# Batch 0's set-up in two halves of the heads, gathers issued earlier, and batch 0's squares and output product moved to the next phase, in a fused attention and snake-activation kernel

## The chip, the cores and the metric

The kernel runs on one core of a Trainium2 chip. The metric is the device time of one execution in microseconds (us). Before the change three runs gave 392.09, 391.79 and 391.86 us, a median of 391.86.

Five engines work side by side, each through its own instructions in order, and wait for each other by semaphores: TensorE (PE in the profile; its weight loads are PEld), VectorE (DVE), ScalarE (ACT), GpSimd (POOL) and SyncE (SP). POOL and SP also issue the transfers (DMAs): POOL those that cast float32 to bfloat16 on the way or that gather rows by an index, SP the others. PE writes its results to PSUM (eight banks of 2 KB on each of 128 partitions); ACT and DVE read them there.

## The reference

```python
# q, k, v: (8 batches, 8 heads, 576 positions, 64); global_idx: 8 sorted positions
scores = scale * np.matmul(q, k.transpose(0, 1, 3, 2))
mask = np.abs(pos[:, None] - pos[None, :]) <= 32          # window
mask = mask | is_global[:, None] | is_global[None, :]     # 8 global positions see and are seen by all
scores = np.where(mask, scores, -1000000000.0)
attn = exp(scores - max); attn = attn / (sum + 1e-09)
x = (attn @ v), heads side by side                        # (4608, 512)
h = x @ w_in                                              # (512, 2048)
s = np.sin(alpha * h)
g = h + s * s / (alpha + 1e-09)
out = g @ w_out                                           # (2048, 512), float32
```

## The kernel before

Everything runs in an order written out by hand; no scheduler moves an instruction. The work goes batch by batch: attention of batch b (`attention`), then the first product with its activation (`gemm1`), and the second product (`gemm2`) spread in single matmuls over the phases behind it, by `fill(n)`: n matmuls of the oldest waiting `gemm2` are put on PE at the place of the call. `phase_a(b+1, b)` is attention of batch b+1 beside the second product of batch b.

*Attention.* 576 positions are 12 tiles of 48. `KX` holds, for each pair of heads and each tile, a 128x128 stationary matrix: the first head's keys in rows and columns 0 to 63, the second's in 64 to 127, zeros elsewhere, and in each half 48 own keys and the 8 global ones. `QX` holds the queries in segments of 52 (4 global, 48 own), with padding; `VX` the values like the keys. All three exist twice, for even and odd batches, and the zeros are written once. For each pair of heads and each group of four tiles `scores` makes four matmuls into a PSUM tile of two (`ring`), ACT takes the exponential (L732) and DVE multiplies by `MASK` (L735). `products` (L766) makes the numerators (with `VX`, into zn) and the denominators (with the blocks of ones `OB`, into zd); `inverse` takes a logarithm L (L792) and an exponential R (L795) on ACT; `sums` reduces the parts of the global queries; `normalise` writes xT (L798). The products of pair hp-1 stand between the scores of pair hp.

*gemm1.* 16 groups nt of 128 columns: eight matmuls (L942), the sine on ACT (L976), its square on ACT or DVE (L981, L983), and H on DVE (L987). The PSUM tiles zn, zr and zd take turns. In batches 0 and 1, groups 10 to 13 also place the next batch's keys and queries (`place`, eight pairs of DVE copies, L348 and L355).

*Set-up of batch 0.* POOL loads k and q of batch 0 as 96 rows (8 heads x 12) of 48x64 values each, with a cast (L443). PE turns them 48 times (L583) into six PSUM tiles of one bank; each tile's copies into `KX` and `QX` (`place_part`, L599 and L604) belong to one engine, ACT or DVE in turn. The rows at the global positions come by three gathers on POOL (L520), with row numbers that DVE computes (`grow`). The mask is made on 64 partitions from small index tiles of POOL, and copied to the other 64 (L570). DVE clears KX[0], ACT QX[0], POOL VX[0] in two halves between the V loads (L525).

*Loads.* On POOL, in this order: V of batch 0, pairs 0 and 1; w_in, row blocks 0 and 1; V, pairs 2 and 3; w_in, blocks 2 and 3; the cast of batch 1's k and q into DRAM (`cast_qk`), which SP later loads turned (`turn_qk`, L338). In batch 0's attention, after pair 0 (`beside(0)`): POOL clears VX[1]; `gather_v` puts eight loads on SP (global rows of V of all batches) and their cast on POOL (L676); `gather_kq` puts eight gathers on POOL (L663), global rows of k and q of all batches; DVE clears KX[1] and QX[1] after pairs 1 and 2 (L1067). `turn_kq` turns the gathered rows on PE ahead of group 9 of batch 0's gemm1 (L684). At group 10 POOL waits (`seen`) for the turned q of batch 1, then loads V of batch 1 with the placing of its globals (L364, L369) behind pair 0, and w_out between pairs 1 and 2. POOL's loads use eight semaphores in turn, so that each waits for the one eight before it.

*Squares.* For a check of the sine's range the kernel sums the squares of x (`square_x`, L873 to L878) and of w_in (`square_w`, L847, L849), on DVE beside the attention of the following batch.

Of the kernel before, what the change touches and what calls it, by code (L numbers as in the profile page):

```python
# [10 lines left out]
ALU = mybir.AluOpType  # L11
# [5 lines left out]
P = 128  # L17
# [230 lines left out]
def kernel(  # L248
# [166 lines left out]
    nat = {w: H2[0:KW, 2 + 3 * w : 5 + 3 * w, :].rearrange("p n c -> p (n c)")[:, 0 : KT * D] for w in (0, 1)}  # L415
    gkq = [H2[:, 14, w * 256 : (w + 1) * 256].rearrange("p (n t d) -> p n t d", n=2, t=2) for w in (0, 1)]
    gv = H2[0 : NG * B, 15, 0 : 2 * H * D].bitcast(DT.float32).rearrange("p (h d) -> p h d", d=D)

    setup = tc.alloc_tile_pool(name="setup", bufs=1)

    g64 = setup.tile([NG * B, 1], DT.int64, name="g64")
    gidx8 = setup.tile([D, NG], DT.int64, name="gidx8")
    gp64 = setup.tile([D, 1], DT.int64, name="gp64")
    for t in (gidx8, gp64):
# [5 lines left out]
    nc.sync.dma_start(out=gp64[KT : KT + NG], in_=global_idx[:, None])  # L430
    nc.sync.dma_start(
        out=gidx8[KT : KT + NG],
        in_=bass.AP(tensor=global_idx.tensor, offset=global_idx.offset, ap=[[0, NG], [1, NG]]),
    )
    nc.sync.dma_start(out=girow[:], in_=global_idx[None, :])
    with nc.allow_non_contiguous_dma("2048 elements once"):
        nc.sync.dma_start(out=alphaT[:], in_=moe_alpha.rearrange("(t p) -> p t", p=P))

    prow = setup.tile([P, 1], DT.int32, name="prow")
    nc.gpsimd.iota(prow[:], pattern=[[0, 1]], base=0, channel_multiplier=1)  # L440
    make_identity(nc, identb[:])
    for w, src in ((1, k), (0, q)):
        nc.gpsimd.dma_start(out=nat[w], in_=src[0].rearrange("h (i r) d -> (h i) (r d)", r=KT))  # L443
    kpos = setup.tile([D, 1], DT.float32, name="kpos")
    odd = setup.tile([D, 1], DT.float32, name="odd")
    nc.gpsimd.memset(odd[:], float(KT - 1))

    nc.gpsimd.iota(kpos[:], pattern=[[0, 1]], base=0, channel_multiplier=2,
                   allow_small_or_imprecise_dtypes=True)
    nc.gpsimd.affine_select(  # L450
        out=odd[:], in_=odd[:], compare_op=ALU.is_ge, fill=0.0, base=-(KT // 2),
        channel_multiplier=1, pattern=[[0, 1]],
    )

    nc.gpsimd.affine_select(
        out=odd[:], in_=odd[:], compare_op=ALU.is_ge, fill=-4096.0, base=KT - 1,
        channel_multiplier=-1, pattern=[[0, 1]],
    )
    nc.gpsimd.tensor_tensor(out=kpos[:], in0=kpos[:], in1=odd[:], op=ALU.subtract)
    qrel = setup.tile([D, 2, 2, WCOL // 2], DT.float32, name="qrel")  # L460
    for par, left in ((0, PAD), (1, 40)):
        nc.gpsimd.iota(qrel[:, par, :, 0:left], pattern=[[1, 2], [2, left]], base=-WIN,
                       channel_multiplier=0, allow_small_or_imprecise_dtypes=True)
        nc.gpsimd.iota(qrel[:, par, :, left:60], pattern=[[1, 2], [2, 60 - left]],
                       base=2 * left - 40, channel_multiplier=0, allow_small_or_imprecise_dtypes=True)
    qpos = setup.tile([D, NT12, 2, 24], DT.float32, name="qpos")
    nc.gpsimd.iota(qpos[:], pattern=[[KT, NT12], [1, 2], [2, 24]], base=0, channel_multiplier=0,
                   allow_small_or_imprecise_dtypes=True)


    later = setup.tile([D, NG], DT.float32, name="later")
    nc.gpsimd.memset(later[:], 0.0)
    nc.gpsimd.affine_select(
        out=later[:], in_=later[:], compare_op=ALU.is_gt, fill=1.0,
        base=-KT, channel_multiplier=1, pattern=[[-1, NG]],
    )
    isg = setup.tile([D, 1], DT.float32, name="isg")
    nc.gpsimd.memset(isg[:], 1.0)
    for base, sgn in ((-KT, 1), (KT + NG - 1, -1)):
        nc.gpsimd.affine_select(  # L480
            out=isg[:], in_=isg[:], compare_op=ALU.is_ge, fill=0.0, base=base,
            channel_multiplier=sgn, pattern=[[0, 1]],
        )
    gi32 = girow[:].bitcast(DT.int32)
    greg = [nc.sync.value_load(gi32[0:1, 2 * j : 2 * j + 1], min_val=0, max_val=S - 1) for j in range(NG)]

    nc.scalar.preload_act_table_set("natural_log_exp_and_others")
    nc.scalar.activation(
        out=QX[0][:].rearrange("p h y c -> p (h y c)"),
        in_=identb[:, 0:1].to_broadcast([P, NHP * 2 * QROW]), func=AF.Copy, scale=0.0,  # L490
    )
    nc.vector.memset(KX[0][:], 0.0)
    rowi = setup.tile([P, 2], DT.int32, name="rowi")
    rowf = setup.tile([P, 4], DT.float32, name="rowf")
    nc.vector.tensor_scalar(out=rowi[:, 0:1], in0=prow[:], scalar1=B - 1, scalar2=None, op0=ALU.bitwise_and)
    nc.vector.tensor_scalar(
        out=rowi[:, 1:2], in0=prow[:], scalar1=NG * B, scalar2=None, op0=ALU.bitwise_and
    )
    nc.vector.tensor_copy(out=rowf[:, 0:2], in_=rowi[:])
    for m in range(2):  # L500
        nc.vector.tensor_copy(
            out=rowf[m * NG * B : (m + 1) * NG * B, 2:3], in_=g64[:].bitcast(DT.int32)[:, 0:1]
        )

    nc.vector.scalar_tensor_tensor(
        out=rowf[:, 3:4], in0=rowf[:, 0:1], scalar=float(S), in1=rowf[:, 2:3], op0=ALU.mult, op1=ALU.add
    )
    nc.vector.tensor_copy(out=grow[:], in_=rowf[0 : NG * B, 3:4])
    nc.vector.memset(ones[:], 1.0)
# [3 lines left out]
    nc.vector.memset(OB[D:P, D:P], 1.0)  # L513


# [19 lines left out]
    nc.scalar.activation(out=qrel[:], in_=qrel[:], func=AF.Square, bias=kpos[:, 0:1], scale=-1.0)  # L535
    band = setup.tile([D, 2, 2, WCOL // 2], DT.bfloat16, name="band")
# [3 lines left out]
    nc.vector.memset(band[0:KT, 0, :, PAD : PAD + 4], 1.0)  # L540
    nc.vector.memset(band[0:KT, 1, :, 40:44], 1.0)
    M2 = MASK[:].rearrange("p (t e) c -> p t e c", e=2)
    nc.vector.tensor_copy(
        out=M2[0:D], in_=band[:].rearrange("p e x c -> p e (x c)")[:, None].to_broadcast([D, 6, 2, WCOL])
    )

    gpf = setup.tile([D, 1], DT.float32, name="gpf")
    nc.vector.tensor_copy(out=gpf[:], in_=gp64[:].bitcast(DT.int32)[:, 0:1])
    nc.scalar.activation(out=qpos[:], in_=qpos[:], func=AF.Square, bias=gpf[:, 0:1], scale=-1.0)
    gf = setup.tile([D, NG], DT.float32, name="gf")  # L550
    nc.vector.tensor_copy(out=gf[:], in_=gidx8[:].bitcast(DT.int32)[:, 0::2])
    first = setup.tile([D, NG], DT.float32, name="first")
    nc.vector.tensor_scalar(
        out=first[:], in0=gf[:], scalar1=gpf[:, 0:1], scalar2=None, op0=ALU.not_equal
    )

    nc.vector.tensor_tensor(out=first[:], in0=first[:], in1=later[:], op=ALU.max)
    fone = setup.tile([D, 1], DT.float32, name="fone")
    nc.vector.tensor_reduce(out=fone[:], in_=first[:], axis=AX.X, op=ALU.min)
    nc.vector.tensor_tensor(out=fone[:], in0=fone[:], in1=isg[:], op=ALU.mult)  # L560
    far = setup.tile([D, NT12, 2, 24], DT.bfloat16, name="far")
# [5 lines left out]
    for e, c0 in ((0, 20), (1, 16)):  # L567
        own = M2[0:D, :, e].rearrange("p t (x c) -> p t x c", x=2)[:, :, :, c0 : c0 + 24]
# [5 lines left out]
    turnp = tc.alloc_tile_pool(name="turnp", bufs=1, space=PSUM)  # L574
    small = tc.alloc_tile_pool(name="small", bufs=1, space=PSUM)
    part, pg = {}, {}
    NA = NH // 3
    for w, name in ((1, "k"), (0, "q")):
        for n in range(3):
            part[w, n] = turnp.tile([P, NA, P], DT.bfloat16, name=f"t{name}{n}")  # L580
            for a in range(NA):
                r = (n * NA + a) * P
                nc.tensor.transpose(  # L583
                    out=part[w, n][:, a, 0:KW], in_=nat[w][:, r : r + P], identity=identb[0:KW, 0:KW]
                )
        pg[w] = small.tile([D, NG * B], DT.bfloat16, name="pg" + name)
        nc.tensor.transpose(
            out=pg[w][:], in_=g0[name][:], identity=identb[0 : NG * B, 0 : NG * B]
        )
    act, dve = nc.scalar.copy, nc.vector.tensor_copy  # L590

    def place_part(w, n, copy):
        for t in range(2):
            rows = slice(t * D, (t + 1) * D)
            for y in range(2):
                src = part[w, n][y * D : (y + 1) * D, :, 0:KW]
                if w == 1:
                    c = t * D + y * NH + n * NA
                    copy(  # L599
                        out=KX[0][rows, :, :, c : c + NA],  # L600
# [99 lines left out]
    def attention(b, beside):  # L700
# [105 lines left out]
        for hp in range(NHP):  # L806
# [4 lines left out]
            if hp:  # L811
                products(hp - 1, (0, 1))
# [340 lines left out]
```

## Time and profile before

| what | value |
|---|---|
| median of three runs | 391.86 us |
| the profiled execution | 392.27 us |
| its span, first to last instruction | 390.5 us |
| PE busy | 340.1 us (87%) |
| DVE busy | 294.6 us (75%) |
| ACT busy | 285.6 us (73%) |
| POOL busy | 137.9 us (35%) |
| mean granted clock of PE | 0.972 |
| batch 0: first scores / first sine | 18.2 / 38.8 us |
| batch 1: first scores / first gemm1 matmul | 63.3 / 85.1 us |
| batch 2: first scores | 108.5 us |

The page cuts the span into 40 slices of 9.76 us; a digit is the busy share of a slice in tenths. A row of the timeline gives start, duration, engine, line, operation, output and inputs, shape, and count; in brackets stands how long the engine was idle ahead of it and what ended that. A row of the windows gives the stretch, its length, PE's busy time (and instructions), the clock that PE was granted as a share of full speed, the DMA engines' share and GB/s. Busy time includes overlapping parts of merged rows, so of matmuls that follow each other the distance between starts tells more than the duration of one.

### The profile page before, as it was taken

The page shows a single profiled execution, that of the slowest core. Times are in us where ns is not written, and L with a number is a line of the kernel's source. Part 1 is how long each engine was busy: PE and PEld are TensorE (multiplying, and loading weights), DVE is VectorE, ACT ScalarE, POOL GpSimd, SP SyncE. Part 2 cuts the span into 40 slices and gives each one's busy share as a digit, 9 for nine tenths or more (in the row PEclk, how much of TensorE's full clock was granted, in tenths as well). Part 3 has the DMA queues.
Part 4 walks back from the last instruction along what each step waited for, and adds up shares of the span by engine and source line. Part 5 has one row for each costly group of instructions (what it writes and reads, how often), then busy time and mean ns, then how long its engine had stood idle before and what let it go on. Part 6 is the DMA issues. An engine that isn't in the chain of part 4 may idle for free. (4 is left out here: it accounts for less than half of the span.)

```text
span 390.5 us, 8393 instructions
## 1 busy us (share of the span) xinstructions
PE 340.1 (87%) x3060; PEld 234.1 (60%) x3107; DVE 294.6 (75%) x599; ACT 285.6 (73%) x552; POOL 137.9 (35%) x219
## 2 busy tenths in 40 slices
PE   2378775999798899999999999999999999899892
PEld 1377543566555576666666666667676766676341
DVE  7967769577969978888888887888788876689400
ACT  6767858668977578778888888788888888675110
POOL 7963795646746600571047203750000000000001
PEclk9985989999999899999999999999999999999997
DMA  7799969999999957488646983644411001101221
GB/s 121 43 163 219 144 47 179 156 150 190 158 140 107 185 108 148 72 77 156 123 71 68 162 127 65 61 56 90 89 44 39 2 27 56 29 2 31 59 75 48
DMA packets 104011, 37.94 MB, mean 97 GB/s; under 512 B 96122, under 2 KB 98170, under 8 KB 103514
## 3 DMA queue, kind: packets, MB, share of 16 engines
q0 software_dynamic: 56224, 18.70, 42.9%
q1 hardware_dynamic: 47738, 18.63, 24.7%
q8 instruction: 26, 0.43, 0.5%
q14 instruction: 23, 0.19, 0.2%
HBM read 37.15 MB, written 17.83 MB: 141 GB/s over the span
## 5 line engine op out<-in xcount | busy, mean ns | idle before, releaser
L1000 PE MATMUL zo<-w_out,H 128*128 128x512 bf16 x529 | 142.3, 379 | 2.7 <-DMA w_out<-in_moe_w_out_dram 0.7
L942 PEld LDWEIGHTS <-w_in 128*128 128x128 bf16 x1024 | 100.5, 99 | 49.7 <-issue 18.5
L386 POOL DMA_DIRECT2D VX<-in_v_dram x128 | 83.5, 664 | 109.3 <-PE zd L766 82.6
L732 ACT ACTIVATE E<-ring 128x480 bf16<-128x480 f32 x96 | 54.3, 568 | 33.7 <-PE ring L724 33.1
L1000 PEld LDWEIGHTS <-H 128*128 128x128 bf16 x576 | 51.8, 97 | 39.2 <-issue 0.8
L942 PE MATMUL zn<-xT,w_in 128*128 128x288 bf16 x384 | 59.2, 292 | 4.8 <-DVE H L987 4.0
L735 DVE TENSOR_TENSOR E<-E,MASK 128x480 bf16<-128x480 bf16 x96 | 36.2, 409 | 19.3 <-ACT E L732 18.1
L942 PE MATMUL zr<-xT,w_in 128*128 128x288 bf16 x320 | 48.9, 289 | 2.0 <-DVE H L987 1.2
L976 ACT ACTIVATE sb<-zn,alphaT 128x576 bf16<-128x576 f32 (+1 forms) x48 | 35.6, 741 | 19.5 <-PE zn L942 15.5
L987 DVE SCALAR_TENSOR_TENSOR H<-s,recipT,zn 128x576 bf16<-128x576 bf16 x48 | 39.1, 814 | 13.3 <-ACT s L981 9.7
L942 PE MATMUL zd<-xT,w_in 128*128 128x288 bf16 x320 | 46.6, 285 | 2.4 <-DVE H L987 2.4
L1028 POOL DMA_INDIRECT out_dram<-osb,grow x1 | 1.0, 1002 | 125.8 <-SPq L1121 125.8
L724 PE MATMUL ring<-QX,KX 128*128 128x120 bf16 x384 | 37.3, 223 | 8.1 <-DVE QX L604 4.5
L981 ACT ACTIVATE s<-sb 128x576 bf16<-128x576 bf16 (+1 forms) x62 | 42.7, 689 | 2.0
L724 PEld LDWEIGHTS <-KX 128*128 128x128 bf16 x384 | 28.2, 101 | 22.5 <-issue 11.2
L987 DVE SCALAR_TENSOR_TENSOR H<-s,recipT,zd 128x576 bf16<-128x576 bf16 x40 | 32.5, 814 | 7.0 <-ACT s L981 5.3
L766 PEld LDWEIGHTS <-VX 128*128 128x128 bf16 x448 | 28.0, 102 | 15.4 <-issue 10.0
L987 DVE SCALAR_TENSOR_TENSOR H<-s,recipT,zr 128x576 bf16<-128x576 bf16 x40 | 32.5, 813 | 4.7 <-ACT s L981 2.4
L983 DVE TENSOR_TENSOR s<-sb 128x576 bf16<-128x576 bf16 (+1 forms) x66 | 30.7, 465 | 6.3 <-ACT sb L976 6.0
L1006 ACT COPY osb<-zo 128x512 f32<-128x512 f32 x36 | 20.8, 578 | 19.9 <-PE zo L1000 19.9
L976 ACT ACTIVATE sb<-zd,alphaT 128x576 bf16<-128x576 f32 (+1 forms) x40 | 29.7, 742 | 7.5 <-PE zd L942 5.1
L766 PE MATMUL zn<-E,VX 128*128 128x120 bf16 (+2 forms) x336 | 28.2, 213 | 6.7 <-DVE xT L798 6.7
(158 smaller groups left out, 449.7 us busy)
## 6 DMA issues: line engine op xcount, KB each, us to landing
VX<-in_v_dram POOLq DMA_DIRECT2D x128, 36.0 KB, 3.3
kd<-in_k_dram POOLq DMA_DIRECT2D x7, 576.0 KB, 9.5
qd<-in_q_dram POOLq DMA_DIRECT2D x7, 576.0 KB, 10.5
w_in<-in_moe_w_in_dram POOLq DMA_DIRECT2D x4, 512.0 KB, 7.4
w_out<-in_moe_w_out_dram POOLq DMA_DIRECT2D x4, 512.0 KB, 9.2
out_dram<-osb SPq DMA_DIRECT2D x8, 256.0 KB
out_dram<-osb SPq DMA_DIRECT2D x8, 224.0 KB
out_dram<-osb SPq DMA_DIRECT2D x8, 192.0 KB
```

The source lines that it names most:

```text
L386: nc.gpsimd.dma_start(out=VX[b % 2][r : r + 24, hp, :, t * D : t * D + D], in_=v[b, 2 * hp + t].rearrange("(i a y) d -> y a i d", a=24, y= ...
L724: nc.tensor.matmul(out=ps[:, e * WCOL : (e + 1) * WCOL], lhsT=kx[:, hp, i, :], rhs=qx[:, hp, :, s0 : s0 + 60], start=True, stop=True, skip ...
L732: nc.scalar.activation(out=Eg, in_=ps[:, 0 : 4 * WCOL], func=AF.Exp, scale=scale, accum_out=EA[:, n : n + 1])
L735: nc.vector.tensor_tensor(out=Eg, in0=Eg, in1=MASK[:, 4 * g : 4 * g + 4, :].rearrange("p i c -> p (i c)"), op=ALU.mult,)
L766: nc.tensor.matmul(out=out_t[:, half, :, a - half * CUT : z - half * CUT], lhsT=OB[:] if key else VXb[:, hp, i, :], rhs=E[:, i, :, a - s0 ...
L942: nc.tensor.matmul(out=h[:, e, 0:HALF], lhsT=lhsT, rhs=xT[:, c, e, :], start=(c == 0), stop=(c == CT - 1), skip_group_check=True,)
L976: nc.scalar.activation(out=sb[:, :, 0:W], in_=h[:, :, 0:W], func=AF.Sin, scale=alphaT[:, nt : nt + 1])
L981: nc.scalar.activation(out=s2[:, :, 0:W], in_=sb[:, :, 0:W], func=AF.Square)
L983: nc.vector.tensor_tensor(out=s2[:, :, 0:W], in0=sb[:, :, 0:W], in1=sb[:, :, 0:W], op=ALU.mult)
L987: nc.vector.scalar_tensor_tensor(out=dst.rearrange("p (e c) -> p e c", e=2), in0=s2[:, :, lo:hi], scalar=recipT[:, nt : nt + 1], in1=h[:, ...
L1000: nc.tensor.matmul(out=ops[:], lhsT=H2[:, nt, blk * P : (blk + 1) * P], rhs=w_out[:, nt, :], start=(nt == 0), stop=(nt == NT - 1),)
L1006: nc.scalar.copy(out=osb[:], in_=ops[:])
```

## The change

Set-up: k and q of batch 0 are loaded and turned in halves of four heads (partitions 0 to 47 and 64 to 111), issued first on POOL. Each half fills 24 columns of 128 rows in two banks (zn, zd, zn again, zo). The first half is placed at once, t = 0 by ACT and t = 1 by DVE; the second by `second_half`, after pair 0's scores, three quarters by ACT. The mask is made on 128 partitions, and its index columns on DVE. VX[0] is cleared by ACT, KX[0] by DVE in halves; alpha comes as 16 rows and is turned on PE. Ten matmuls of ones are put ahead of the first transposes.

Loads: the gathers of batch 0 stand right behind the index tiles; w_in comes in four blocks of 512 columns; the cast of batch 1 stands between the second and third. After pair 0 POOL clears QX[1], and `gather_kq` stands ahead of the cast of the values and of the clearing of VX[1]; DVE clears KX[1] in four pieces. `seen` reads the turned k, and V of pairs 1 and 2 of batch 1 goes ahead of w_out.

Attention: in batch 0 the denominators of a pair stand ahead of scores(hp, 2) and the numerators behind it. A matmul of ones follows each group of scores of pairs 1 to 3 of batch 0 and 0 to 2 of batch 1. In batch 1 `fill` puts its matmuls (64 in all) behind pair 3 and into gemm1, and the squares of batch 0's x and of two row blocks of w_in go to groups 3, 4, 6 and 8 of batch 1's gemm1.

```diff
-    def load_w_in(cs):
-        for c in cs:
-            nc.gpsimd.dma_start(out=w_in[:, c, :], in_=moe_w_in[c * P : (c + 1) * P, :])
+    def load_w_in(gs):
+        for g in gs:
+            cols = slice(g * DFF // 4, (g + 1) * DFF // 4)
+            nc.gpsimd.dma_start(
+                out=w_in[:, :, cols], in_=moe_w_in[:, cols].rearrange("(c p) n -> p c n", p=P)
+            )
...
+    for half in range(2):
+        for w, src in ((1, k), (0, q)):
+            nc.gpsimd.dma_start(
+                out=nat[w][D * half : D * half + HK],
+                in_=src[0, HH * half : HH * half + HH].rearrange("h (i r) d -> (h i) (r d)", r=KT),
+            )
...
-    for w, src in ((1, k), (0, q)):
-        nc.gpsimd.dma_start(out=nat[w], in_=src[0].rearrange("h (i r) d -> (h i) (r d)", r=KT))
...
+    clear(QX[0][:].rearrange("p h y c -> p (h y c)").bitcast(DT.float32))
...
+    clear(vflat[:, 0:half])
...
+    def warm(z, n):
+        for _ in range(n):
+            nc.tensor.matmul(
+                out=z[:], lhsT=ones[:], rhs=ones[:][:, None, :].to_broadcast([P, 4, P]),
+                start=True, stop=True, skip_group_check=True,
+            )
+    warm(zo[0], 10)
...
-    for hps in ((0, 1), (2, 3)):
-        nc.gpsimd.memset(VX[0][:, hps[0] : hps[1] + 1].bitcast(DT.int32), 0)
-        if hps[0] == 0:
-            load_v(0, hps)
-    load_w_in((0, 1))
-    load_v(0, (2, 3))
-    load_w_in((2, 3))
-    cast_qk(1)
+    nc.scalar.activation(out=qrel[:], in_=qrel[:], func=AF.Square, bias=kpos[:, 0:1], scale=-1.0)
+    clear(vflat[:, half : 2 * half])
+    load_v(0, (0,))
+    load_w_in((0,))
+    load_v(0, (1, 2))
+    load_w_in((1,))
+    load_v(0, (3,))
+    cast_qk(1)
+    load_w_in((2, 3))
     load_vg(0)
...
+    def turn_part(w, half, z):
+        part[w, half] = z[:].bitcast(DT.bfloat16)[:, :, 0 : NH // 2 * HK].rearrange("p n (a c) -> p n a c", c=HK)
+        rows = slice(D * half, D * half + HK)
+        for a in range(NH):
+            nc.tensor.transpose(
+                out=part[w, half][:, a // 12, a % 12], in_=nat[w][rows, a * P : (a + 1) * P],
+                identity=identb[rows, rows],
+            )
...
+    turn_part(1, 0, zn)
+    for y in range(2):
+        place_part(1, 0, 0, y, act)
+        place_part(1, 0, 1, y, dve)
+    turn_part(0, 0, zd)
+    gpf = setup.tile([P, 1], DT.float32, name="gpf")
...
     nc.scalar.activation(out=qpos[:], in_=qpos[:], func=AF.Square, bias=gpf[:, 0:1], scale=-1.0)
+    for y in range(2):
+        place_part(0, 0, 0, y, act)
+        place_part(0, 0, 1, y, dve)
...
+    turn_part(1, 1, zn)
...
+    turn_part(0, 1, zo2)
+    for t, copy in ((0, act), (1, dve)):
+        place_global_keys(t, copy)
+        place_global_queries(t, copy)
+    nc.vector.tensor_copy(out=alphaT[:], in_=both[:, 0:NT])
...
-    nc.vector.tensor_copy(out=MASK[D:P], in_=MASK[0:D])
...
+    def second_half():
+        for w in (1, 0):
+            for t, y, copy in ((0, 0, act), (0, 1, act), (1, 0, act), (1, 1, dve)):
+                place_part(w, 1, t, y, copy)
...
+        def idle(hp):
+            if (b == 0 and hp) or (b == 1 and hp < 3):
+                warm(zo[0], 1)
...
                 scores(hp, g)
                 fill(per_scores[hp][g])
-            if hp:
+                idle(hp)
+            if b == 0 and hp:
+                products(hp - 1, range(3), (1,))
+            elif hp:
                 products(hp - 1, (0, 1))
             scores(hp, 2)
+            idle(hp)
+            if b == 0 and hp:
+                products(hp - 1, range(3), (0,))
+            elif hp:
+                products(hp - 1, (2,))
             if hp:
-                products(hp - 1, (2,))
                 inverse(hp - 1)
...
+            if b == 1 and nt in (3, 4):
+                square_x(0, nt - 3)
+            if b == 1 and nt in (6, 8):
+                square_w(nt // 2 - 3)
             if b == 0 and nt == 10:
-                nc.gpsimd.tensor_copy(out=seen[:], in_=turned[1][0][0:1, 0:1])
+                nc.gpsimd.tensor_copy(out=seen[:], in_=turned[1][1][0:1, 0:1])
                 load_v(1, (0,))
                 place_globals(1)
-                load_v(1, (1,))
+                load_v(1, (1, 2))
                 load_w_out()
-                load_v(1, (2, 3))
+                load_v(1, (3,))
...
-            fill(PER_GROUP[nt])
+            fill((GROUP_LATE if b == 1 else PER_GROUP)[nt])
...
-    LATE = ((0, 0, 0), (2, 6, 4), (6, 6, 6), (6, 6, 8))
+    LATE = ((0, 0, 0), (0, 0, 0), (0, 0, 0), (4, 4, 6))
     MIDST = 4
     PER_GROUP = (0, 0, 5) + 11 * (1,) + (0, 0)
+    GROUP_LATE = (0, 0, 4) + 10 * (3,) + (4, 4, 4)
...
                 if at == 0:
-                    nc.gpsimd.memset(VX[1][:].bitcast(DT.int32), 0)
+                    second_half()
+                    nc.gpsimd.memset(QX[1][:].bitcast(DT.int32), 0)
                     gather_v()
                     gather_kq()
+                    cast_globals_v()
+                    nc.gpsimd.memset(VX[1][:].bitcast(DT.int32), 0)
                     turn_qk(1)
-                if 1 <= at < 3:
-                    nc.vector.memset((KX, QX)[at - 1][1][:], 0.0)
+                if at >= 0 and at < NHP:
+                    nc.vector.memset(KX[1][:, at], 0.0)
                 return
...
-            if 0 <= at < 2:
+            if 0 <= at < 2 and b_moe:
                 square_x(b_moe, at)
...
-            if b_moe < 2 and at in (2, 3):
-                square_w(2 * b_moe + at - 2)
+            if b_moe == 1 and at in (2, 3):
+                square_w(at)
```

More of the change, by code (lines that the diff above doesn't have):

```diff
@@ L450 @@
[L450 to L482, printed above, removed]
+    nc.sync.dma_start(out=girow[:], in_=global_idx[None, :])
+    arow = setup.tile([NT, P], DT.float32, name="arow")
+    for t in (0, D):
+        nc.sync.dma_start(out=gp64[t + KT : t + KT + NG], in_=global_idx[:, None])
+        nc.sync.dma_start(
+            out=gidx8[t + KT : t + KT + NG],
+            in_=bass.AP(tensor=global_idx.tensor, offset=global_idx.offset, ap=[[0, NG], [1, NG]]),
@@ L545 @@
     )
-    gpf = setup.tile([D, 1], DT.float32, name="gpf")
+    small = tc.alloc_tile_pool(name="small", bufs=1, space=PSUM)
+    both = small.tile([P, 512], DT.float32, name="pg")
+    act, dve = nc.scalar.copy, nc.vector.tensor_copy
+    part = {}
+    def turn_part(w, half, z):
[5 more added lines that the diff above has]
+                identity=identb[rows, rows],
+            )
@@ L577 @@
[L577 to L588, printed above, removed]
-        )
@@ L689, in turn_kq @@
             )
-    banks = mctx.enter_context(tc.tile_pool(name="banks", bufs=1, space=PSUM))
-    zn, zd = [banks.tile([P, 2, 512], DT.float32, name=name) for name in ("zn", "zd")]
-    zo = [banks.tile([P, 512], DT.float32, name=f"zo{i}") for i in range(2)]
     xTs = {}
```

236 lines of the change are left out of this document (133 added, 103 removed).

## The prediction

> **What bounds the kernel now.** I read the page's forty slices first, then the waits of TensorE (PE), then the timeline of the first 110 us engine by engine.
>
> ```profile
> PE   2378775999798899999999999999999999899892
> DVE  7967769577969978888888887888788876689400
> ACT  6767858668977578778888888788888888675110
> PEclk9985989999999899999999999999999999999997
> ```
>
> From the fifteenth slice (137 us) to the last but two PE is at nine tenths nearly throughout, and from the twelfth (107 us) never under eight: there PE's work counts, and the change leaves batches 2 to 7 as they are. What it can win or lose lies before 110 us, and a shift there goes through to the end.
>
> The first wait that the change aims at is that for batch 0's queries (columns of the timeline: start, busy time, engine, line, what; in brackets the idle time ahead and what ended it):
>
> ```profile
> 7.52 2.10 PE L583 MATMUL tk<-identb,H 96*128 96x96 bf16 x24 [7.52 <-DMA H<-in_k_dram]
> 8.38 3.87 ACT L599 COPY KX<-tk 64x384 bf16<-64x384 bf16 x8
> 13.56 4.54 DVE L604 COPY QX<-tq 64x384 bf16<-64x384 bf16 x8
> 15.21 1.03 ACT L623 COPY QX<-pgq 64x112 bf16<-64x112 bf16 x4
> 18.20 0.96 PE L724 MATMUL ring<-QX,KX 128*128 128x120 bf16 x8 [4.55 <-DVE QX L604]
> 23.98 0.73 ACT L792 ACTIVATE L<-zd,tiny 128x576 f32<-128x576 f32 x1
> 38.81 0.74 ACT L976 ACTIVATE sb<-zn,alphaT 128x576 bf16<-128x576 f32 x1 [0.25 <-PE zn L942]
> ```
>
> k is in at 7.5, first scores at 18.2, the first logarithm L (head pair 0 done) at 24.0, batch 0's first sine at 38.8. The second is the gathered rows of batches 1 to 7:
>
> ```profile
> 37.90 0.60 POOL L676 CAST VGb<-H 64x512 bf16<-64x512 f32 x1 [6.02 <-DMA H<-in_v_dram]
> 48.11 0.94 POOL L663 DMA_INDIRECT H<-in_q_dram,gsrc  x1 [0.30 <-issue]
> 50.71 0.22 PE L684 MATMUL zo<-identb,H 128*128 128x128 bf16 x1 [2.43 <-DMA H<-in_q_dram,gsrc]
> 52.85 0.74 ACT L976 ACTIVATE sb<-zn,alphaT 128x576 bf16<-128x576 f32 x1 [3.73 <-PE zn L942]
> 54.34 0.81 DVE L987 SCALAR_TENSOR_TENSOR H<-s,recipT,zn 128x576 bf16<-128x576 bf16 x1 [2.89 <-ACT s L981]
> ```
>
> The cast sat 6.0 us on POOL for SP's loads, the eight gathers queued behind it, and the last came 2.4 us late for PE. The third is the clock (stretch, length, PE busy, granted clock, DMA):
>
> ```profile
> 26.50:27.00 0.50, 0.50 (x14) 0.94 1.61 121
> 27.00:27.50 0.50, 0.50 (x12) 0.50 1.23 79
> 37.50:38.00 0.50, 0.50 (x6) 1.00 0.53 111
> 51.00:51.50 0.50, 0.50 (x4) 0.50 1.12 68
> ```
>
> After 1.8 us without a matmul (24.5 to 26.3) PE runs at half clock for ten us, through all of batch 0's attention; after the 2.4 us at 48.3 for 3.5 us more.
>
> **The set-up (to batch 0's first sine): +2.3 us.** *Arrival.* Four loads replace two, issued at 1.0 instead of 1.6. k took 5.9 us from issue; q, equally large, landed 2.7 us behind it, so half of k saves 1.4: it lands at 5.5. Ten warming matmuls (128x512; gemm2's follow each other by 0.215 at full clock, so 0.43 at half) fill PE to about then. 24 transposes took 2.1 us with 96 columns; with 48 between 1.05 and 2.1, I take 1.4: k's half is turned at 6.9. All of what follows lies beside the load: POOL loses ten small mask operations (0.9 us at 2.85, 0.9 at 4.97) and both clearings of VX (1.4 each), which ACT does before 6.7 in two pieces around the square of qrel; DVE gets a dozen small operations (0.1 to 0.15 each) and the mask on 128 partitions (the same durations), and loses the mask's second copy (1.53). If ACT or DVE ran late here, the copies would start later by as much; DVE, done by about 8.0, has nothing to spare.
>
> *Copies.* In before each bank's copies belong to one engine, and ACT (13.27) and DVE (13.56) overlap. Now both read the same two-bank tile, and in the built program they wait for each other in turn: ACT two, DVE two, ACT two, DVE two. A copy has 288 elements: ACT's 0.258 (112) and 0.484 (384) give 0.40; DVE's 0.567 (384) shrinks to 0.43 to 0.47, I take 0.44. With four hand-overs of 0.1 one operand takes 2x(0.80+0.88+0.2) = 3.8; k and q 7.6. Between them DVE casts gpf and ACT squares qpos (0.13+0.78), after them come seven small DVE operations (1.3 by L551 to L560), then the globals (0.57+2x0.26) and alpha's copy (0.1). 6.9+7.6+0.9+1.3+1.1+0.1 = 17.9: first scores 0.3 earlier than 18.2. The Trainium skill's page "PSUM — Partial Sum Buffer", section "PSUM bank collisions raise a hardware error", has it that two engines must be kept apart by bank and quadrant, and by it these waits are needed; without them copies would run side by side and first scores come some 3.6 us sooner. The trace of before agrees, as its overlapping copies are of different banks.
>
> *Second half of the heads.* It follows head pair 0's exponentials, which end 2.5 us after first scores (18.2 to 20.7 before), at 20.4. ACT copies 12x0.40 = 4.8, then DVE's last two: 26.2. Queued behind it on ACT are head pair 1's exponentials; on PE a warming matmul into zo waits for those last reads, and behind it stand scores(1,1) and the products. Then 0.43 (warming) +0.4+0.2 to exp(1,1) at 27.2 (21.5 before), 0.43+1.3+0.4+0.3 for warming, products and scores to exp(1,2), its 0.6, and L at 29.9: +5.9.
>
> *Rounds.* From L to the sine before took 14.8 us: rounds of 5 to 5.5 at half clock, with DVE's clearing of KX (2.62) in between. New: denominators ahead of numerators, so PE no longer stands waiting for xT; KX cleared in four pieces of 0.66. ACT then needs 3x0.56 + 0.75 + 0.70 = 3.13 a round; PE at full clock 2.6. I take 3.4: L and R 1.45, two rounds 6.8, last L and R 1.45, table 1.3, hand-overs 0.2: 11.2, and 41.1 against 38.8. Bounds: +0.5 (transposes 1.05, rounds 3.13, DVE 0.43) to +5.9 (rounds as before).
>
> **The gathers: -3.2.** On POOL after the first three gathers (ending about 9): 16 V loads x 0.66, four w_in loads and two casts at about 0.6 = 14.1, clearing QX[1] (1.2, from DVE) to 24.5, eight gathers at 1.25 to 34.5, the last two held (a load waits for the one eight before it) until the last w_in pieces land: 39 at the latest, as batch 1's casts, last in that line before, let SP go on at 38.1. They are in by 42 and wanted at 50: covered by 8 us, and if they came later than that the 2.4 would be back. Then group 9 starts at 48.3 instead of 50.76 and takes 1.14 instead of 2.05: 2.4+0.8 = 3.2; bounds 2.4 (PE's idle time alone) and 3.7 (ACT's). Behind them on POOL the cast (0.6) and VX[1]'s clearing (2.7) end by 43, before batch 1's globals. SP's queue: small index loads in new order, alpha as one 16-row load, then as before; nobody waits for it before 9. The copy "seen" waits for kt instead of qt, which lands first. w_in in column blocks: issued at 12.5, 18, 22 and 23, wanted at 40 and then every four groups; 7.4 us to landing. V of head pairs 1 and 2 (8x0.66) goes ahead of w_out, whose issue follows batch 1's globals by 5.3 instead of 2.6; with four loads of some 3 us each it is in about 10 us after batch 1's attention begins, and wanted first there at 8 to 9, piece by piece: hidden, by little. If not, gemm2's first matmuls wait up to 1 us, in a stretch where PE has that to spare.
>
> **Batch 1's attention and gemm1: -0.3.** 36 of gemm2's 54 matmuls (0.215 each, 7.7 us) and the squares of x and two of w_in (1.27+1.5+1.2+2.4 = 6.4 us of DVE) go from attention to gemm1; nine warming matmuls come in (1.9). Attention's rounds were 6.2 and 5.8, filled by PE; without fills the chain products, exp, L, R, xT remains, 67.87 to 72.0 = 4.2. 1.1 (pair 0's products no longer behind six fills) +2.0+1.6+0.3 = 5.0 saved. gemm1: thirty more fills cost PE 6.5 of which about 3.3 lie in its idle stretches (0.5 to 0.7 each); DVE's chain from the third H on is 13x0.735 + 4x0.555 + places 4.3 + squares 6.4 = 22.4 without a gap, ending 4.5 later than now; ACT's table then waits for the last group: +4.7 taken. Bounds +3.2 (squares fit) and +6; attention -5.5 and -2.6.
>
> Sum: 2.3-3.2-0.3 = -1.2 us. The profiled execution took 392.27 (span 390.5, 1.8 around), 0.4 above the median of 391.86; so 391.1 as profiled, **390.7** at the median.
>
> **Rivals.** *Slower: the half clock.* Rows: 1.8 us of idle PE were enough at 24.5; in batch 0 PE idles 6 us while the second half is copied (20.4 to 26.2), and batch 1's rounds keep 1.5 us free each. For it: the rows above. Against: batch 1's attention kept clock 1.00 with 2.4 us idle in 62.4 to 65.9, and PE is dense from 26.2 to 32. If batch 0's rounds stay cold, +3.6; batch 1's, 0.8 in each of three, +2.4. It decides from 1.2 us. Time 394.3 to 396.7, middle 395. The Trainium skill's page "TensorE: Matmul & The Clock Gate", section "Why this matters for your kernels", allows gaps up to about 3 us; by it batch 1's rounds stay at full clock (no 2.4), but the 1.8 us row contradicts it, and the row decides.
>
> *A larger gain.* Rounds of 3.13 and the low bounds of the set-up (+0.5), the stall's 3.7, and squares fitting into gemm1 (-5.0+3.2 = -1.8): -5.0, 386.9. Against: DVE's 22.4 without a gap.
>
> *No net change.* The later sine (+2.3, or 3 with DVE at 0.47) eats the gathers' 3.2: 391.9.
>
> **How the numbers follow.** The sum's case 0.36, the larger gain 0.15, no net change 0.15, half clock 0.34. The range reaches to 386.0, below the larger gain, and to 395.5, past the middle of the cold case, leaving out some 0.05 and 0.12. What a measurement can tell from no change is about 0.2%, 0.8 us: faster 0.51, same 0.15, slower 0.34. The likeliest case's own range is 388 to 391.
>
> **What would show it.** Right: first scores near 18, a gap of some 6 us in PE behind them, ACT's twelve copies in it, L near 30, the sine near 41; turn of the gathered rows without a wait; batch 1's attention about 17 us, its gemm1 about 28. Wrong: first scores by 15, or a sine before 39; clock 0.50 past 34 us or in batch 1's attention; PE waiting for w_out, V or w_in.

## The result and the profile after

The kernel after took 445.4 us at the median of four; the kernel before took 392.0 beside it. Without one disturbed execution of 454.1 the four lie between 442.8 and 446.5, and the ratio to the kernel before is 1.134, with a 95% interval of 1.128 to 1.140: 13% slower, where the prediction had 0.3% faster. The profiled execution took 442.8 us, its span is 441.1 against 390.5. The slices of the page after:

```profile
PE   5468968788796988997988887699879878798784
DVE  6657895499479878777487847387648753588300
ACT  6579987657666686878577855588658855675111
PEclk8559999999999999999899998899989999999998
```

PE used to be at nine tenths from the fifteenth slice on. Now it falls to six, seven and eight again and again up to the end, and DVE and ACT fall with it: no other engine has become the bound. One row of the waits of the whole run names what stops PE (engine, line, what it waited for: total us, times, longest):

```profile
PE zo L1055 <- ACT osb L1061: 46.7, 35, 3.5
```

L1055 is gemm2's matmul, L1061 ACT's copy of a finished 128-row block of the output from `zo` to `osb`. gemm2 makes 36 blocks of 16 matmuls, so there are 35 changes from one block to the next; at every one of them PE waits, 0.2 to 3.5 us, 1.33 on average. In the kernel before no such row exists; the groups of the two kernels (busy, mean ns, then idle time ahead and what ended it), first before (its trace has records of 529 of the 576 matmuls, so its 142.3 is too low):

```profile
L1000 PE MATMUL zo<-w_out,H 128*128 128x512 bf16 x529 | 142.3, 379 | 2.7 <-DMA w_out<-in_moe_w_out_dram 0.7
```

and after:

```profile
L1055 PE MATMUL zo<-w_out,H 128*128 128x512 bf16 x576 | 163.0, 391 | 46.7 <-ACT osb L1061 46.7
```

One such change in the timeline of after, ACT and then PE (start, busy time, engine, line, what; idle time ahead):

```profile
252.38 1.28 ACT L748 ACT_TABLE_LOAD   x1
253.67 0.58 ACT L1061 COPY osb<-zo 128x512 f32<-128x512 f32 x1
```

```profile
254.31 0.38 PE L1055 MATMUL zo<-w_out,H 128*128 128x512 bf16 x1 [2.75 <-ACT osb L1061]
254.53 0.37 PE L764 MATMUL ring<-QX,KX 128*128 128x120 bf16 x4
```

The copy itself takes 0.58, but ACT does its work in order, and here a table load of 1.28 stood ahead of it. PE stands for 2.75 us, and the scores queued behind gemm2's matmul stand with it.

Consecutive blocks use different banks (`ops = zo[(blk + b // 2) % 2]`), so that PE can fill one while ACT empties the other. What changed is a pair of lines that neither the change's description above nor the diff above shows:

```diff
-    zo = [banks.tile([P, 512], DT.float32, name=f"zo{i}") for i in range(2)]
+    zo2 = banks.tile([P, 2, 512], DT.float32, name="zo")
+    zo = [zo2[:, i, :] for i in range(2)]
```

The second half of q's transposes wanted a tile of two banks, and so `zo[0]` and `zo[1]` became two slices of one. The program's waits are made by tile, not by bank: the built program after lets the first matmul of each block wait for the copy of the block before it, out of the other bank, as the rows above show.

The loss grows with the number of blocks. First scores of each batch (us), and the difference:

| batch | 0 | 1 | 2 | 3 | 4 | 5 | 6 | 7 | span |
|---|---|---|---|---|---|---|---|---|---|
| before | 18.2 | 63.3 | 108.5 | 152.7 | 193.1 | 233.2 | 273.4 | 312.5 | 390.5 |
| after | 18.2 | 62.1 | 114.3 | 160.7 | 204.6 | 254.5 | 304.2 | 350.0 | 441.1 |
| later by | 0 | -1.3 | 5.7 | 8.0 | 11.5 | 21.3 | 30.8 | 37.5 | 50.6 |

Up to batch 1's first scores the change had won 1.3 us; gemm2 begins behind them. The steps of that stretch in the timeline of after, beside which the lines of the prediction for before can be laid:

```profile
7.28 1.05 PE L581 MATMUL zn<-identb,H 48*128 48x48 bf16 x24 [2.37 <-DMA H<-in_k_dram]
8.37 0.69 ACT L594 COPY KX<-zn 64x288 bf16<-64x288 bf16 x2 [1.57 <-PE zn L581]
9.09 0.82 DVE L594 COPY KX<-zn 64x288 bf16<-64x288 bf16 x2 [1.52 <-ACT KX L594]
9.93 0.69 ACT L594 COPY KX<-zn 64x288 bf16<-64x288 bf16 x2 [0.88 <-DVE KX L594]
18.16 0.98 PE L764 MATMUL ring<-QX,KX 128*128 128x120 bf16 x8 [3.88 <-DVE alphaT L666]
25.80 0.61 PE L533 MATMUL zo<-ones 128*128 128x512 bf16 x1 [5.16 <-DVE QX L599]
39.79 0.94 POOL L705 DMA_INDIRECT H<-in_q_dram,gsrc  x1 [2.39 <-DMA w_in<-in_moe_w_in_dram]
40.79 0.74 ACT L1031 ACTIVATE sb<-zn,alphaT 128x576 bf16<-128x576 f32 x1 [0.23 <-PE zn L993]
49.79 0.39 PE L728 MATMUL zo<-identb,H 128*128 128x128 bf16 x4
```

ACT and DVE copy in turn (8.37, 9.09, 9.93), the second half holds PE for 5.2 us up to 25.80, the first sine is at 40.79, and the gathered rows are turned at 49.79 without a wait.

### The profile page after: what moved, and what is told of

Its sections match the earlier page's. It is cut to its first block, busy times and chain, and to the rows that moved or that the text cites. A ratio compares the mean times of both kernels' runs of the same rounds, so it can differ in the third digit from the quotient of the medians.

```text
span 441.1 us, 8617 instructions
## 1 busy us (share of the span) xinstructions
PE 356.7 (81%) x3184; PEld 236.5 (54%) x3184; DVE 293.4 (67%) x616; ACT 289.8 (66%) x559; POOL 139.0 (32%) x211
## 5 line engine op out<-in xcount | busy, mean ns | idle before, releaser
L1055 PE MATMUL zo<-w_out,H 128*128 128x512 bf16 x576 | 163.0, 391 | 46.7 <-ACT osb L1061 46.7
L993 PEld LDWEIGHTS <-w_in 128*128 128x128 bf16 x1024 | 99.3, 97 | 52.3 <-issue 20.7
L1055 PEld LDWEIGHTS <-H 128*128 128x128 bf16 x576 | 53.7, 100 | 79.0 <-issue 44.7
L775 DVE TENSOR_TENSOR E<-E,MASK 128x480 bf16<-128x480 bf16 x96 | 37.1, 408 | 44.9 <-ACT E L772 43.7
L993 PE MATMUL zn<-xT,w_in 128*128 128x288 bf16 x384 | 57.3, 285 | 4.3 <-DVE H L1042 4.0
L993 PE MATMUL zr<-xT,w_in 128*128 128x288 bf16 x320 | 47.9, 285 | 2.3 <-DVE H L1042 1.3
L993 PE MATMUL zd<-xT,w_in 128*128 128x288 bf16 x320 | 46.6, 285 | 2.1 <-DVE H L1042 1.9
L764 PEld LDWEIGHTS <-KX 128*128 128x128 bf16 x384 | 29.1, 103 | 27.9 <-issue 14.2
L764 PE MATMUL ring<-QX,KX 128*128 128x120 bf16 x384 | 38.4, 226 | 6.5 <-DVE alphaT L666 3.9
L1061 ACT COPY osb<-zo 128x512 f32<-128x512 f32 x36 | 20.8, 578 | 27.2 <-PE zo L1055 27.1
L1031 ACT ACTIVATE sb<-zr,alphaT 128x576 bf16<-128x576 f32 (+1 forms) x40 | 29.6, 740 | 7.5 <-PE zr L993 6.3
L806 PEld LDWEIGHTS <-VX 128*128 128x128 bf16 x448 | 26.4, 100 | 13.8 <-issue 7.0
```

Source lines behind the costliest of these rows:

```text
L764: nc.tensor.matmul(out=ps[:, e * WCOL : (e + 1) * WCOL], lhsT=kx[:, hp, i, :], rhs=qx[:, hp, :, s0 : s0 + 60], start=True, stop=True, skip ...
L775: nc.vector.tensor_tensor(out=Eg, in0=Eg, in1=MASK[:, 4 * g : 4 * g + 4, :].rearrange("p i c -> p (i c)"), op=ALU.mult,)
L806: nc.tensor.matmul(out=out_t[:, half, :, a - half * CUT : z - half * CUT], lhsT=OB[:] if key else VXb[:, hp, i, :], rhs=E[:, i, :, a - s0 ...
L993: nc.tensor.matmul(out=h[:, e, 0:HALF], lhsT=lhsT, rhs=xT[:, c, e, :], start=(c == 0), stop=(c == CT - 1), skip_group_check=True,)
L1031: nc.scalar.activation(out=sb[:, :, 0:W], in_=h[:, :, 0:W], func=AF.Sin, scale=alphaT[:, nt : nt + 1])
L1055: nc.tensor.matmul(out=ops[:], lhsT=H2[:, nt, blk * P : (blk + 1) * P], rhs=w_out[:, nt, :], start=(nt == 0), stop=(nt == NT - 1),)
```

## The experiments

The runs fell on three chips, named B, C and D here; A is the chip of the two profiles above. On B and C the kernel before took 397 us and on D 393, against 392 on A, so each run is compared with the kernel before on its own chip.

**One tile in the kernel before (B).** The pair of lines above, put into the kernel before and nothing else.

> The kernel before with one edit: gemm2's two accumulators zo[0] and zo[1] are the two banks of one PSUM tile instead of two tiles. Theory (the shared tile): in the kernel after, the first matmul of 35 of gemm2's 36 blocks waits for ACT's copy of the block before it, 46.7 us in all, though it writes the other bank. This edit alone should then cost nearly the whole difference: 45 to 52 us, so 437 to 444 us, with some 35 waits of PE zo on ACT osb of 40 to 50 us in all. Rival (the rest of the set-up is the cause: warming matmuls, moved fills, other loads): the edit changes nothing, 392 us within 1 us.

It took 446.0 us against 397.0: ratio 1.124 (1.117 to 1.132), 49 us, as expected; the 437 to 444 were reckoned from the 392 of A. The row of waits:

```profile
PE zo L1001 <- ACT osb L1007: 43.3, 34, 3.5
```

The two lines alone make 49 of the 53 us that the change cost on A; the rest of the change is not needed for it.

**Two tiles in the kernel after (B, C, D).** The reverse: `zo2` in a pool of its own, given back after batch 0's attention.

```diff
+    turnp = tc.alloc_tile_pool(name="turnp", bufs=1, space=PSUM)
-    zo2 = banks.tile([P, 2, 512], DT.float32, name="zo")
+    zo2 = turnp.tile([P, 2, 512], DT.float32, name="zo")
...
     phase_a(0, None)
+    turnp.release()
+    zop = mctx.enter_context(tc.tile_pool(name="zop", bufs=1, space=PSUM))
+    zo = [zop.tile([P, 512], DT.float32, name=f"zo{i}") for i in range(2)]
```

> The kernel after with one edit: once batch 0's attention is through, the two-bank tile zo is given back, and gemm2 gets two tiles of one bank each, as in the kernel before. All else of the change stays. Theory (the shared tile): the 46.7 us of waits go, and what is left is what the prediction summed, -1.2 us against the kernel before: 390 to 391 us, 386 to 395 at the outside. In the trace of after batch 0's last sine already starts at 61.2 instead of 62.4. Rival (another part costs the time): it stays over 430 us.

398.9 us against 397.0 (B): ratio 1.005 (1.002 to 1.008), 2 us slower, where 1.2 faster was expected. The row of waits is gone, and gemm2's group has no idle time:

```profile
L1056 PE MATMUL zo<-w_out,H 128*128 128x512 bf16 x576 | 153.6, 380 | 0.0
```

Of the 53 us lost on A all but 2 are back on B. The same 576 matmuls also keep PE busy for some 9 us less than in after (163.0) or in one_zo (162.5): there some of the waits were followed by 3.4 us at half clock. After the wait of 2.35 us that ended at 208.42, the windows of after (stretch, length, busy PE, PEld, DVE, ACT and POOL, granted clock, DMA):

```profile
208.00:208.50 0.50, 0.08 (x1) 0.07 (x1) 0.47 (x2) 0.37 (x1) 0.00 (x0) 1.00 0.00 0
209.00:209.50 0.50, 0.50 (x3) 0.15 (x2) 0.00 (x0) 0.00 (x0) 0.00 (x0) 0.50 0.47 123
```

The Trainium skill's page "PSUM — Partial Sum Buffer", section "PSUM bank collisions raise a hardware error", asks for a guard between engines on the same bank and the same group of partitions. By it a matmul into one bank needs no wait for a copy out of the other, and this run, which has none, agrees.

**Two tiles from batch 4 on (C).** The kernel after, with the exchange only ahead of batch 4's attention.

> The kernel after, with zo exchanged for two one-bank tiles only ahead of batch 4's attention: 13 of gemm2's 36 blocks still share one tile. Theory (each block change costs its wait): the loss up to there stays, 12 waits instead of 35. In the trace of after, batch 4's first scores come 11.5 us later than in the kernel before; from there on nothing more is lost: 11 to 15 us over the kernel before, ratio 1.028 to 1.038. Rival (a loss that does not go by the number of block changes, as a slower clock): over 1.08. Its set-up is that of after to the instruction, so its trace also shows whether ACT's two late starts of two_zo belong to the set-up.

414.9 us against 397.5: ratio 1.046 (1.039 to 1.054), 18.4 us, above the expected 11 to 15.

```profile
PE zo L1056 <- ACT osb L1062: 15.3, 13, 3.1
```

13 waits of 1.2 us. Against the trace of the kernel before on the same chip, batch 4's first scores come 15.1 us later, batch 5's 17.7, batch 7's 17.3, and the span ends 15.4 later: the loss stops soon after the tile is exchanged. 13 of the 35 changes cost 18.4 of some 50 us, so the loss goes by the number of block changes. The edit does one thing more: it puts all of gemm2's waiting matmuls on PE ahead of the exchange (`while waiting: fill(1)`), so that batch 4's first scores start 2.1 us behind batch 3's last sine (213.61 and 211.50) instead of with it, as in the kernel before (198.53 and 198.52). That and the 1 to 2 us that two_zo loses on B and C are of the size of the excess; the run does not divide it.

**The gathers alone (C).** In the kernel before:

```diff
-        nc.gpsimd.tensor_copy(out=VGb[:], in_=gv.rearrange("p h d -> p (h d)"))
...
-                    nc.gpsimd.memset(VX[1][:].bitcast(DT.int32), 0)
                     gather_v()
                     gather_kq()
+                    nc.gpsimd.tensor_copy(out=VGb[:], in_=gv.rearrange("p h d -> p (h d)"))
+                    nc.gpsimd.memset(VX[1][:].bitcast(DT.int32), 0)
```

> The kernel before with one part of the change: in batch 0's attention the eight gathers are issued by POOL ahead of the cast of the gathered values and of the clearing of VX[1], instead of behind them. The prediction has -3.2 us for the gathers (2.4 idle time of PE and 0.8 of half clock; bounds 2.4 and 3.7). Theory: the gathers start near 30 instead of 39, the transposes of the gathered rows wait for nothing, and the end comes 2.4 to 3.7 us sooner, ratio 0.991 to 0.994. Rival (what is late next takes it back, as the keys' and queries' loads or the values behind them on the queue): under 1 us.

394.3 us against 397.5: ratio 0.991 (0.988 to 0.994), 3.5 us faster (2.3 to 4.8). The first gather starts at 29.6, and the rows are turned at 49.14 without a wait. This small reorder alone is faster than the kernel before.

**The moves around batch 1 (B).** two_zo with the fills, squares, warming matmuls of batch 1 and the load order put back.

```diff
-    LATE = ((0, 0, 0), (0, 0, 0), (0, 0, 0), (4, 4, 6))
+    LATE = ((0, 0, 0), (2, 6, 4), (6, 6, 6), (6, 6, 8))
...
-            fill((GROUP_LATE if b == 1 else PER_GROUP)[nt])
+            fill(PER_GROUP[nt])
...
```

> As two_zo, and with the moves around batch 1 undone: gemm2(0)'s fills mostly in batch 1's attention again, the squares of x of batch 0 and of w_in there too, no warming matmuls in batch 1, w_out loaded before the values of head pair 2. The prediction's sum has -0.3 us for these moves (attention -5.0, gemm1 +4.7; bounds -2.3 to +3.4): 0.3 us slower than two_zo by the sum, with batch 1's attention about 5 us longer and its gemm1 about 5 us shorter. Rival (squares fit into gemm1's idle stretches): 1.5 to 2.5 us slower than two_zo. Rival (the moves cost time): 1 to 3 us faster than two_zo.

399.0 us beside two_zo's 398.9: the moves are worth nothing measurable. From batch 1's first scores to batch 2's it takes 46.4 us with them back and 46.6 without. The parts moved as expected: attention with its table load to the first sine 25.9 against 19.0, gemm1 20.5 against 27.7.

**One engine to a tile (B).** two_zo, with ACT copying all of k and DVE all of q in the set-up.

```diff
-    for y in range(2):
-        place_part(1, 0, 0, y, act)
-        place_part(1, 0, 1, y, dve)
+    for t in range(2):
+        for y in range(2):
+            place_part(1, 0, t, y, act)
...
```

The other lines of the edit give q's copies to DVE, behind its small operations, and the rows at the global positions and alpha to ACT, and share the second half of the heads evenly (eight copies each instead of twelve and four).

> As two_zo, but each two-bank tile of the set-up is read by one engine: ACT copies all of k, DVE all of q, in both halves of the heads (in the kernel after ACT and DVE read the same tile in turn and wait for each other). The prediction has 3.6 us at first scores for these waits. Theory (the turns cost this): k's and q's copies run side by side, first scores at about 14.6 instead of 18.2, the second half done at about 21 instead of 25.8, and the end 3.5 to 5 us earlier than in two_zo: 385 to 387 us. Rival (something else is late next, as the w_in columns or the gathered rows): first scores come earlier, but the end moves by less than 1.5 us.

394.2 us against two_zo's 398.9: 4.6 us, as expected; against the kernel before 0.993 (0.990 to 0.997). The two operands now run side by side:

```profile
10.17 2.79 ACT L595 COPY KX<-zn 64x288 bf16<-64x288 bf16 x8 [3.37 <-PE zd L582]
10.52 3.33 DVE L600 COPY QX<-zd 64x288 bf16<-64x288 bf16 x8
16.41 0.96 PE L767 MATMUL ring<-QX,KX 128*128 128x120 bf16 x8 [0.77 <-ACT alphaT L668]
```

First scores come at 16.4 instead of 19.9, and PE is held for the second half until 22.91 instead of 27.54. The copies of k and q end 3.7 us after the first of them starts (10.17 to 13.85) instead of 7.3 (10.10 to 17.42), which is the gain at first scores; the other 1.1 us come in the second half, where the even sharing counts too. It is the same fault in small: two engines wait for each other because they read one tile.

**The remaining 3 us: another trace of both kernels (C).** two_zo should have been 1.2 us faster than before and was 2 us slower. In its trace ACT twice starts work late whose input was ready.

> two_zo once more, for a trace beside the one of the kernel before from the same chip. In its first trace ACT began the set-up's copies 1.7 us late (at 10.1, with the transposes done at 8.4) and one exponential 1.8 us late (at 37.0, its scores done at 35.2), and batch 0's first sine came at 45.6 instead of the predicted 41.1. Theory A (a property of the program): both delays come again, sine near 45.6. Theory B (this one execution or this chip): they are gone or elsewhere, sine near 41, and the run is 1 us faster than the kernel before.

> The kernel before, unchanged, for a trace from the same chip as the runs beside it. In the runs so far the kernel before took 397.0 us (393.3 to 399.3) on the chip of the first experiments and 391.9 on the chip of its first profile. Expected: batch 0's first sine near 39 and batch 1's first scores near 63 on any chip; if a chip is slower as a whole, all stretches are longer alike.

These were written as if C were B. The kernel before took 397.8 us, two_zo 398.5. Batch 0's first sine is at 39.1 in the kernel before, as expected, but batch 1's first scores are at 66.3 instead of near 63. Both show late starts, the kernel before at another place. Before, on C:

```profile
51.46 0.74 ACT L976 ACTIVATE sb<-zn,alphaT 128x576 bf16<-128x576 f32 x1 [4.66 <-remote]
```

two_zo on B:

```profile
10.10 0.69 ACT L595 COPY KX<-zn 64x288 bf16<-64x288 bf16 x2 [3.30 <-PE zd L582]
36.99 0.57 ACT L773 ACTIVATE E<-ring 128x480 bf16<-128x480 f32 x1 [2.95 <-remote]
```

swap_mid on C:

```profile
10.19 0.69 ACT L595 COPY KX<-zn 64x288 bf16<-64x288 bf16 x2 [3.39 <-remote]
```

"remote" means that no instruction in the profile released it. At 51.46 the sums had been finished at 45.97; at 10.10 the transposes of zn had been finished at 8.4, and at 36.99 the scores at 35.15. The row at 10.10 names the transposes of zd (to 9.81), which this copy does not read; in swap_mid the same copy starts at 10.19, while the last of them run (10.10 to 10.35), and no releaser is named. Batch 0's first sine is at 45.6 (B) and 47.4 (C) in two_zo, so that the set-up costs 8.3 us on C instead of 2.3 (6.9 in swap_mid, where the sine is at 45.95). Theory A holds for these two chips. It is not the program alone: swap_mid, whose set-up is that of after, has both late starts, and after on A has neither.

**The set-up put back, and two_zo once more (D).** The kernel before with the gathers ahead and batch 1's moves, which is two_zo without the new set-up (and without what else the change does up to batch 0's gemm1: w_in by columns, the new order of the products, KX[1] cleared in pieces); two_zo beside it.

> The kernel before with the gathers ahead (as gathers_first) and with the moves around batch 1 (gemm2's fills, the squares, nine warming matmuls, the load order), but with its own set-up. What is missing against two_zo is the set-up anew alone. By the prediction's terms: -3.2 and -0.3, 3.5 us faster than the kernel before, and 2.3 us faster than two_zo. By the traces of the second chip, in which batch 0's first sine comes 6.5 to 8.3 us later with the new set-up: 5.5 to 6 us faster than two_zo, so that the set-up is the term that was mis-sized there.

> two_zo beside setup_back on the same chip. If the chip is that of the first experiments: 1.5 to 2.5 us slower than the kernel before, with ACT's late starts at 10.1 and near 37. If ACT starts its first copy at 8.4 (as in the trace of after on its own chip): 1 to 2 us faster than the kernel before.

Against the kernel before (393.3): setup_back 0.996 (0.992 to 1.000), 1.7 us faster; two_zo 0.997 (0.993 to 1.0005), 1.2 us faster. On D ACT starts its first copy at 8.66:

```profile
8.66 0.69 ACT L595 COPY KX<-zn 64x288 bf16<-64x288 bf16 x2 [1.86 <-PE zn L582]
```

The first sine is at 41.1 with the new set-up and at 38.8 with the old: 2.4 us. At the end the two differ by 0.4 us, less than the intervals can tell, and setup_back fell short of its 3.5; the kernel before itself scatters from 390.6 to 396.5 on D. (The profiled execution of two_zo on D took 400.1 us, and only its first 45 us are read here.)

**Fewer transfers early (D).** two_zo, with the second halves of k and q loaded behind the small gathers.

> As two_zo, with the loads of the second halves of k and q issued behind the three small gathers (near 9.5 instead of 2.7), to see whether ACT's late first copy (10.1 to 10.3 in six traces of one chip, 8.4 in the trace of after on another, its transposes done at 8.4 in both) comes from transfers in flight at the time. Theory (contention): with half as much in flight ACT starts by 8.6. Rival (it has nothing to do with these transfers): it starts at 10.1 again. The second halves are turned later, which costs some 3 us in any case.

392.3 us in its one execution, first copy at 8.18. Since two_zo on the same chip had no late start either, this decides nothing. The traces that the expectation speaks of were five, on B and C.

## Why the prediction was wrong

The step that failed is in the first paragraph: "the change leaves batches 2 to 7 as they are". It left their loops as they are, but not the tile that gemm2 works in. The sum holds no term for it, no rival names it, and so the range ended some 50 us below the time. The knowledge was there: the paragraph on the copies says that ACT and DVE wait in turn because they read the same two-bank tile, and the one on the second half says that PE's warming matmul into zo waits for those reads. Both take the shared tile for a matter of the set-up; the question of who else uses `zo` later was not asked. The missing term could have been estimated: 35 changes, at each ACT's queue, then its copy (0.58 in the trace of before) and the hand-over. In after each came to between 0.2 and 3.5 us, 46.7 in all.

What the sum did contain, term by term:

- *Set-up, +2.3.* The size is right on A (+2.0, sine at 40.79 for 41.1) and D (+2.4), and the waits that the prediction names are there. First scores at 18.16 for 17.9 were luck, though, as two errors cancelled. k's half was turned from 7.28 to 8.33, not done by 6.9, for it was in 1.8 us later than taken: +1.4. The eight copies of an operand took 3.1 us, not 3.8: -1.3 for k and q. Behind them PE was held until 25.80 (26.2), and L came at 29.38 (29.9; the steps given for it add up to 30.3). The low bound of +0.5 does not follow from its three terms either, which give about +1.3. And the prediction calls ACT's and DVE's waits needed because the engines must be kept apart by bank and quadrant; by that premise only part of them are. ACT's second pair of copies (at 9.93) reads partitions 64 to 127 and waits for DVE's first pair (at 9.09), which reads 0 to 63. No run here leaves that wait out. On B and C, with ACT's late starts, the set-up cost 6.8 to 8.3 (on B against one_zo, which has the old set-up).
- *Gathers, -3.2.* Right: batch 0's last sine starts at 61.21 instead of 62.41, so the stretch behind the first sine is 3.2 us shorter on A; alone it is worth 3.5 (2.3 to 4.8) on C, where the trace of the kernel before has its late start in just this stretch, so that not all of it need be the gathers. The last gather was issued at 39.79 ("39 at the latest").
- *Batch 1, -0.3.* Right in sum, mis-sized in its parts: between the two traces of C attention saves 7.4 instead of 5.0 and gemm1 costs 6.8 instead of 4.7, -0.6 in all; between fills_back and two_zo on B it is +0.2, and the end does not show it. DVE's squares of w_in (1.45 and 1.77 behind each other) make PE wait for H in gemm1; two_zo on B:

```profile
104.25 1.14 PE L994 MATMUL zd<-xT,w_in 128*128 128x288 bf16 x8 [2.33 <-DVE H L1043]
```

- *Sum, -1.2.* Without the shared tile it comes out on D (-1.2, between -2.6 and +0.2) and not on B (+2.0), where ACT's late starts stand, which no row of before on A showed. On D it is in part luck: the gathers and batch 1's moves gave 1.7 instead of 3.5, and the set-up took back 0.4 instead of 2.3.
- *The half clock* (the slower rival) was right for the stretch after the idle PE and no longer. Windows of after:

```profile
20.00:26.00 6.00, 0.84 (x6) 0.43 (x5) 2.75 (x9) 5.38 (x17) 5.23 (x9) 0.50 1.51 190
26.00:31.00 5.00, 5.00 (x45) 3.97 (x44) 2.24 (x7) 2.81 (x8) 4.12 (x4) 0.50 0.89 186
31.00:36.00 5.00, 4.69 (x74) 3.93 (x73) 3.88 (x9) 4.47 (x14) 3.03 (x3) 0.97 1.22 190
```

The clock is full again from 31 on, as the sum had assumed for the rounds. Direction and size were wrong all the same, and the chance of 0.34 for slower was given to this rival, not to what happened.

## What to carry to other kernels

When a change joins two PSUM buffers into one tile, or slices one that was two, list every later user of it, however far from the edit: waits are made by tile, and a double buffer whose halves share a tile is no double buffer (1.33 us at each of 35 changes here). Compare the waits of the built programs, line by line, on the lines that the diff does not touch. Two engines that copy out of one tile take turns; give each a tile of its own.

## What was not expected of the hardware

- In all eight traces from chips B and C an engine (mostly ACT) is held at least once in the first 55 us with no releaser in the profile, up to 5.5 us after its input was ready; in the five traces from A and D no such row stands in this stretch. Whether code, transfers or something else holds the engine is open: late_halves fell on a chip without it.
- The gap after which the clock halves is not fixed by its length: after waits of 2.27 and 2.35 us (ending at 269.72 and 208.42) half clock followed for 3.4 us, after 2.75 and 3.10 (at 254.31 and 81.15) it stayed full, and the durations agree: four scores matmuls took 0.37 at 254.53, against 0.61 at half clock at 26.20. The Trainium skill's page "TensorE: Matmul & The Clock Gate", section "Why this matters for your kernels", allows gaps up to about 3 us; the two shorter ones contradict it. The windows of after behind the wait of 2.75:

```profile
254.50:255.00 0.50, 0.50 (x7) 0.35 (x6) 0.20 (x1) 0.07 (x1) 0.00 (x0) 1.00 0.00 0
255.00:255.50 0.50, 0.50 (x7) 0.35 (x6) 0.00 (x0) 0.50 (x3) 0.00 (x0) 1.00 0.73 197
```
